# PSUM rings, emission order and first loads of an FFT filter with a mixture of experts behind it

## The chip, the cores and the metric

One core of one Trainium2 chip. The metric is the device time of one execution in microseconds (us); the time before is the median of three runs, 1523.91 us (1520.41 to 1524.9). The profile is of one more execution, of 1515.94 us.

## What is computed

The reference, cut to what matters:

```
x: (8, 2496, 256); filt_r, filt_i: (1249, 256); w_gate: (256, 8); w1: (8, 256, 1024); w2: (8, 1024, 256)
X = np.fft.rfft(x, axis=1)
Y = X * (filt_r + 1j * filt_i)
t = np.fft.irfft(Y, n=2496, axis=1).reshape(19968, 256)
logits = t @ w_gate
e = argmax(logits, axis=1); p = softmax(logits)[e]
out[row] = p * (relu(t[row] @ w1[e]) @ w2[e])       # for each row, its own expert
```

A filter by circular convolution along the sequence, then one expert of eight for each row of the result.

## The kernel before, in words

**The stages.** The sequence length is split as 2496 = 39 x 64, so a DFT is two small ones. The work of the first stage is cut into 16 units (u = 2 * batch + half of the 256 channels), and a unit into 5 steps, 80 steps t in all. `forward1(u, j)` (line 250; j = 0 to 5, six banks of columns) multiplies input columns by the 39-point table and leaves the result in T. A step is `spec1` (291, four transposes), `spec2` (305, the 64-point DFT), `filt_` (323, the product with the filter, on VectorE), `join` (336, real and imaginary parts, two instructions on GpSimd and two on VectorE) and `spec3` (348, the inverse 64-point DFT, copied to U by ScalarE).

When both units of a batch are through, the batch is **routed** (lines 481 to 614): `route1` and `route1b` take the gate's product twice (s = 0, 1), turn it round and copy it out on VectorE; `route2` to `route6` are a chain of small matmuls, exponentials, one-hot rows and prefix sums that ends in each row's place (`dest`) and its gate weight (`meta`). And it is **inverted**: for j = 0 to 10, `inv1` transposes (618) and ScalarE rounds the result (gh), `inv1b` takes the rest on VectorE (gq, 635), `inv2` multiplies three times into one PSUM bank and ScalarE copies it out (yt, 649 to 651), and `inv3` (654) adds the meta columns and scatters two groups of rows to the dispatch buffer xs with GpSimd.

Beside this, 16 chunks of **expert weights** are loaded, scaled and split in two f16 halves: `w_load`, `w_max` (VectorE), `w_turn` (a matmul), `w_top` (VectorE), `w_wide` (a matmul), `w_scale`, `w_hi` (ScalarE), `w_lo` (VectorE), `w_out` (to memory). The second stage (from line 912) runs the experts over blocks of 128 rows; `layer1` and `layer2` are its matmuls. It needs all the weights, and the rows dispatched so far.

**The order.** Nothing is scheduled by a tool: each call is entered with `at(key, f, ...)` (803), the list is sorted by key (1125), and the engines' queues are filled in that order. Each engine takes its own instructions strictly in that order. The unit of the keys is one step: `spec1(t)` has the key t, `spec2` t + 1.394, `spec3` t + 3.6. Line 821 has the distances, with `w` the key of the first weight chunk and `wp` the distance to the next. `RT` (822) has the ten links of the routing, counted from s0, the moment the batch is complete. The inverse begins `lead` after s0 and has a pair each 0.75 steps, with `inv1b` 0.4 and `inv2` 0.9 after `inv1`, and `inv3` 1.2 after it (times c, which is 0.6 in the last batch). The weights, the constants and x are loaded by SP's queue (`loadx` is 3 DMAs, `loadf` 8, or 12 for the first); lines 753 to 772 and then the list fill it.

**PSUM.** There are 8 banks. Pools turn round: an allocation waits until the tile that had the bank before has been read. Before, pF has 4 banks for forward1, spec1, spec2, spec3 and inv1; pY has 2 for inv2; pW has 1 for w_turn and w_wide; pD has 1 for the routing. In the last batch inv2 uses pF.

Of the kernel before, what the change touches and what calls it, by code (L numbers as in the profile page):

```python
# [9 lines left out]
F32 = mybir.dt.float32  # L10
# [7 lines left out]
PSUM = bass.MemoryType.PSUM  # L18
# [95 lines left out]
def tile_fft_moe(ctx, tc, x, filt_r, filt_i, w_gate, w1, w2, cst, out):  # L114
    nc = tc.nc
    B = x.shape[0]
# [7 lines left out]
    SEG = []  # L124
# [60 lines left out]
    with ExitStack() as fctx:  # L185
# [6 lines left out]
        wp = pool(name="wp", bufs=2)  # L192
        fp = pool(name="fp", bufs=1)
        rp = pool(name="rp", bufs=1)
        pF = pool(name="pF", bufs=4, space=PSUM)
# [2 lines left out]
        sctx = fctx.enter_context(ExitStack())  # L198
        early = lambda **k: sctx.enter_context(tc.tile_pool(reuse_waits="tile", **k))
        sp = early(name="sp", bufs=2)  # L200
        pY = early(name="pY", bufs=2, space=PSUM)
        pW = early(name="pW", bufs=1, space=PSUM)
        pA = pB = pC = pF

        cm = kp.tile([128, 20, 128], F32, name="cm")
        bm = kp.tile([128, 20, 128], F32, name="bm")
# [43 lines left out]
        def forward1(u, j):  # L250
            g0, g1 = BANKS[j]
            n = 0
            ps = pC.tile([128, 512], F32, name=f"f1_{u}_{j}", tag="pF")
            for g in range(g0, g1):
                m = GP if g < NG - 1 else N1
                nc.tensor.matmul(  # L256
                    ps[:, n : n + m],
                    lhsT=xt.pop((u, g))[:m],
                    rhs=a1[:m, :m],
                    start=True,  # L260
                    stop=True,
                )
                n += m
            (nc.scalar.copy if j in (0, 1, 2, 3, 5) else nc.vector.tensor_copy)(  # L264
                T[u % 2].rearrange("p r n -> p n r")[:, 3 * g0 : 3 * g0 + n // N1, :],
                ps[:, :n].rearrange("p (n r) -> p n r", r=N1),
            )
# [140 lines left out]
        def w_turn(e, i):  # L408

            wf, m = whs[e, i]  # L410
            ps = pW.tile([128, 512], F32, name=f"pw{e}_{i}", tag="pW")
            nc.tensor.matmul(ps[0:1, :128], lhsT=m[:, 2:3], rhs=ident, start=True, stop=True)
            whs[e, i] = (wf, m, ps)

# [3 lines left out]

        def w_wide(e, i):
            wf, m, ps = whs[e, i]  # L420
            ps = pW.tile([128, 512], F32, name=f"pv{e}_{i}", tag="pW")
            nc.tensor.matmul(ps[:, 0:1], lhsT=one, rhs=m[0:1, 0:1], start=True, stop=True)
            whs[e, i] = (wf, ps)

# [341 lines left out]
        ps = pD.tile([128, 512], F32, name="pwarm", tag="pD")  # L766
        for i in range(7):
            nc.tensor.matmul(ps, lhsT=warm[:, :128], rhs=warm, start=True, stop=True)
        for j in range(6):
            forward1(0, j)  # L770
            if j < 2:
                loadx(0, j + 4)
# [30 lines left out]
        def at(key, f, *a):  # L803
            work.append((key, f, a))
# [13 lines left out]
                    )  # L818


        K = {"s2": 1.394, "sr": 1.65, "si": 1.85, "s3": 3.6, "f": 0.063, "fd": 0.75, "w": 2.0, "wp": 4.3}
        RT = (0.0, 0.4, 0.45, 0.9, 1.3, 1.7, 2.2, 2.5, 2.9, 3.3)
        slow = lambda t: min(1.0, max(0.6, 1.0 - 0.06 * (t - 72)))
        for t in range(NT):
            u, it = divmod(t, 5)
            rho = slow(t)
            at(t, spec1, t)
            at(t + K["s2"] * rho, spec2, t)
            at(t + K["sr"] * rho, filt_, t)
            at(t + K["si"] * rho, join, t)  # L830
            at(t + K["s3"] * rho, spec3, t)
            if 0 < t < 5:
                at(max(t - 1.8, 0.05), loadf, t)
            if u + 1 < NU_ALL and it == 0:
                for j in range(6):
                    at(t + K["f"] + K["fd"] * j, forward1, u + 1, j)
            if u + 1 < NU_ALL and it == 0:
                for j in range(6):

                    n = 6 * (u + 1) + j - 4  # L840
                    v, i = divmod(n, 6)
                    at(5 * (v - 1) + K["f"] + K["fd"] * i + 0.02 if v else 0.01 + 0.02 * i, loadx, u + 1, j)
        for i in range(1, 5):
            if i > 1:
                at(0.1, loadk, bm, "bm", i, i + 1)
            at(0.1, loadk, cm, "cm", i, i + 1)

        PLACE = (80.0, 89.2, 109.2)
        done = []
        for b in range(B):  # L850
            rho = slow(10 * b + 9)
            s0 = 10 * b + 9 + K["s3"] * rho + 0.05
            c = 1.0 if b < B - 1 else 0.6
            for i, f in enumerate(
                (
                    (route1, 0),
                    (route1b, 0),
                    (route1, 1),
                    (route1b, 1),
                    (route2,),  # L860
                    (route3,),
                    (route4,),
                    (route4b,),
                    (route5,),
                    (route6,),
                )
            ):
                at(s0 + c * RT[i], f[0], b, *f[1:])
            lead = 2.0 if b < B - 1 else 1.3


            t = 10 * b + 20
            d = 0.35
            if b < B - 1:
                z = PLACE[0] - 2.85 if b == B - 2 else t + K["s3"] * slow(t) - 0.15
                d = min(0.75, (z - s0 - lead) / (NPAIR - 1))
            for j in range(NPAIR):
                z = s0 + lead + j * d
                at(z, inv1, b, j)
                at(z + 0.4 * c, inv1b, b, j)  # L880
                at(z + 0.9 * c, inv2, b, j)
                z = max(z + 1.2 * c, s0 + c * RT[9] + 0.1 + 0.9 * d * j)
                at(z, inv3, b, j)
            if b in [r for r, _, _ in SEG]:
                for s, v in enumerate(SEG):
                    if v[0] == b:
                        at(s0 + c * RT[9] + 0.2 + 0.1 * s, finish, s)
            done.append(z)
        for q in range(2 * E):
            e, i = divmod(q, 2)  # L890
            z = K["w"] + K["wp"] * q
            at(max(z - 3.2, 0.2 + 0.3 * q), w_load, e, i)
            for d, f, *a in (
                (0.0, w_max, 0),
                (0.12, w_max, 1),
                (0.9, w_turn),
                (1.0, w_top),
                (1.5, w_wide),
                (1.65, w_scale),
                (1.75, w_hi, 0),  # L900
                (1.85, w_hi, 1),
                (2.05, w_lo, 0),
                (2.2, w_lo, 1),
                (3.0, w_out),
            ):
                at(z + d, f, e, i, *a)
# [172 lines left out]
        for s, (r, m, n) in enumerate(SEG):  # L1079
            n *= m  # L1080
            a = PLACE[s]
            z = PLACE[s + 1] if s + 1 < len(SEG) else a + 0.5 * n
# [21 lines left out]
        for k in range(nu):  # L1104
            s, i, m, b0 = units[k]
            z, d, _ = tau[b0]
# [3 lines left out]
        for b in range(NB):  # L1110
            z, d, s = tau[b]
            y = max(opened(s) + 0.3, z - 1.1)
# [67 lines left out]
```

## Time and profile before

| | us |
|---|---|
| median of three runs | 1523.91 (1520.41 to 1524.9) |
| the profiled execution | 1515.94 |
| its span on the core | 1514.2 |
| what lies around the span | 1.74 |
| first step (spec1) at | 19.7 |
| sixth step (first of the second unit) at | 52.7 |
| last step (t = 79) at | 566.0 |
| mean granted TensorE clock | 0.959 |

The times of steps are the starts of their transposes (line 296) in the timeline. The profile names engines PE (TensorE matmuls), PEld (its weight loads), DVE (VectorE), ACT (ScalarE), POOL (GpSimd) and SPq (SP's DMA issues). A view of waits sums the idle time of one engine just before a group of its instructions and names what ended it; a windows view gives the busy time of each engine in a stretch.

### The profile page before, as it was taken

The numbers are of one execution on the slowest core, as the hardware profiler recorded it, in microseconds if no ns is written. First come the engines' busy times: TensorE is split into PE (matmuls) and PEld (weight loads), VectorE is DVE, ScalarE is ACT, GpSimd is POOL, SyncE is SP. The second block draws the span as 40 slices with busy tenths as digits, with TensorE's granted clock in tenths as the row PEclk, the third lists the DMA queues.
The fourth block names the chain that finished last, engine by engine and source line by source line (L and its number), as shares of the span: only waits on it lengthen the run. The fifth ranks groups of instructions, "written<-read, shape, count | busy, mean of one in ns | idle before, by whom it ended". The sixth has DMA issues, their size and how long they took to land.

```text
span 1514.2 us, 41597 instructions
## 1 busy us (share of the span) xinstructions
PE 1361.8 (90%) x15559; PEld 1212.1 (80%) x15559; DVE 879.1 (58%) x2550; ACT 850.0 (56%) x1440; POOL 480.7 (32%) x525
## 2 busy tenths in 40 slices
PE   6889888887888968679999998999999999999997
PEld 4767677676776747558999998899999899999997
DVE  0888777786768644535555554455555455555553
ACT  2457565655565544345656665566566566565664
POOL 1235565555554653442111111111111111111111
PEclk7899999999898998889999999999999999999999
DMA  6745444454443242227737339933733634534531
GB/s 182 217 143 164 149 149 130 150 164 140 129 151 120 60 163 65 83 69 191 197 79 181 81 76 306 264 77 75 184 76 100 155 80 123 136 77 96 164 77 44
DMA packets 200120, 199.19 MB, mean 132 GB/s; under 512 B 104707, under 2 KB 178100, under 8 KB 191724
## 3 DMA queue, kind: packets, MB, share of 16 engines
q1 hardware_dynamic: 180396, 153.80, 36.9%
q0 software_dynamic: 19520, 42.71, 10.1%
q8 instruction: 124, 2.03, 0.6%
q14 instruction: 80, 0.66, 0.1%
HBM read 347.54 MB, written 61.56 MB: 270 GB/s over the span
## 4 chain that ended last, share of the span: by engine, by line
PE 44%; DMA 4%; SPq 3%; issue 2%; DVE 1%; ACT 1%; POOL 0%; POOLq 0%; DVEq 0%
PE ph L1026 22%; PE po L1052 21%; DMA wb<-wscr 2%; DMA wa<-wscr 1%; SPq L935 1%; SPq L1013 1%; SPq L973 0%; DVE hl L1040 0%; POOL out_dram L158 0%; DMA xt<-xs 0%; SPq L943 0%; ACT hs L1032 0%; ACT hh L1034 0%; ACT xs L1005 0%; DVE xs L1006 0%
## 5 line engine op out<-in xcount | busy, mean ns | idle before, releaser
L1026 PE MATMUL ph<-xt,wa 128*128 128x128 f16 x7728 | 467.7, 220 | 22.2 <-issue 10.6
L1026 PEld LDWEIGHTS <-wa 128*128 128x128 f16 x7728 | 449.9, 99 | 34.3 <-issue 16.8
L1040 DVE TENSOR_TENSOR hl<-hs,hh 128x512 f16<-128x512 f32 x322 | 222.8, 692 | 370.7 <-ACT hh L1034 314.0
L1052 PE MATMUL po<-wb,hh 128*128 128x256 f16 x2576 | 431.7, 273 | 6.9 <-DMA wb<-wscr 3.7
L158 POOL DMA_INDIRECT out_dram<-ot,t x161 | 158.0, 982 | 693.7 <-DVE xs L1006 610.1
L1052 PE MATMUL po<-wb,hl 128*128 128x256 f16 x1288 | 351.1, 273 | 0.4 <-issue 0.4
L1052 PEld LDWEIGHTS <-hh 128*128 128x128 f16 x2576 | 244.8, 98 | 36.2 <-issue 5.8
L1032 ACT ACTIVATE hs<-ph 128x512 f32<-128x512 f32 x322 | 191.8, 596 | 107.8 <-PE ph L1026 93.1
L158 POOL DMA_INDIRECT xs<-yt,dest x176 | 185.1, 1052 | 109.9 <-issue 31.7
L1005 ACT ACTIVATE xs<-xb,s 128x256 f16<-128x256 f32 x161 | 81.8, 508 | 228.0 <-DVE s L995 223.2
L1034 ACT CAST hh<-hs 128x512 f16<-128x512 f32 x322 | 199.0, 618 | 10.2
L1052 PEld LDWEIGHTS <-hl 128*128 128x128 f16 x1288 | 126.0, 98 | 16.3 <-issue 1.3
L361 ACT COPY U<-pi 128x512 f32<-128x512 f32 (+1 forms) x80 | 87.6, 1095 | 91.5 <-PE pi L356 52.2
L256 PE MATMUL f<-a,x 117*128 117x117 f32 x704 | 109.1, 300 | 14.5 <-DMA x<-in_x_dram 12.7
L356 PE MATMUL pi<-cm,p 128*128 128x128 f32 (+1 forms) x640 | 98.6, 297 | 24.6 <-POOL p L345 13.4
L256 PEld LDWEIGHTS f<-a,x 117*128 117x128 f32 x704 | 99.9, 211 | 25.8 <-issue 12.7
L1006 DVE SCALAR_TENSOR_TENSOR xs<-xb,s,xs 128x256 f16<-128x256 f32 x161 | 78.5, 488 | 65.1 <-ACT xs L1005 55.2
L356 PEld LDWEIGHTS pi<-cm,p 128*128 128x128 f32 x640 | 85.2, 202 | 37.5 <-issue 18.5
L264 ACT COPY T<-f 128x468 f32<-128x468 f32 (+1 forms) x80 | 70.8, 885 | 58.7 <-PE f L256 56.7
L314 PE MATMUL px<-z,bm 128*64 128x128 f32 x1280 | 96.7, 298 | 3.0 <-ACT U L361 2.7
L345 POOL TENSOR_TENSOR p<-tr,ti 64x256 f32<-64x256 f32 x80 | 62.8, 785 | 107.3 <-DMA xs<-yt,dest 104.0
L344 POOL TENSOR_TENSOR p<-tr,ti 64x256 f32<-64x256 f32 x80 | 62.7, 784 | 104.8 <-DVE ti L331 95.0
(171 smaller groups left out, 1476.9 us busy)
## 6 DMA issues: line engine op xcount, KB each, us to landing
wb<-wscr SPq DMA_DIRECT2D x134, 1040.0 KB
wa<-wscr SPq DMA_DIRECT2D x134, 1024.0 KB
xb<-xs SPq DMA_DIRECT2D x161, 130.0 KB
x<-in_x_dram SPq DMA_DIRECT2D x240, 78.0 KB
wf<-in_moe_w_dram SPq DMA_DIRECT2D x32, 512.0 KB
wscr<-wh SPq DMA_DIRECT2D x8, 1040.0 KB
wscr<-wh SPq DMA_DIRECT2D x8, 1024.0 KB
xs<-yt,dest POOLq DMA_INDIRECT x176
```

Source lines behind the costliest of these rows:

```text
L158: nc.gpsimd.indirect_dma_start(out=dst, out_offset=bass.IndirectOffsetOnAxis(ap=idx, axis=0), in_=src, in_offset=None, bounds_check=bound, ...
L256: nc.tensor.matmul(ps[:, n : n + m], lhsT=xt.pop((u, g))[:m], rhs=a1[:m, :m], start=True, stop=True,)
L314: nc.tensor.matmul(ps[64 * a : 64 * a + 64, i, j], lhsT=bm[:, 4 * it + kk, 64 * i : 64 * i + 64], rhs=z[:, kk], start=True, stop=True,)
L356: nc.tensor.matmul(ps[:, o : o + n], lhsT=p[:, kk], rhs=cm[:, k, :n], start=True, stop=True)
L361: nc.scalar.copy(U[u % NU].rearrange("p n r -> p r n")[:, r0 : r0 + o // 64, :], ps[:, :o].rearrange("p (r n) -> p r n", n=N2),)
L1005: nc.scalar.activation(xs_[:, 0], xb[:, :D], AF.Copy, scale=sc)
L1006: nc.vector.scalar_tensor_tensor(xs_[:, 1], xb[:, :D], sc, xs_[:, 0], op0=ALU.mult, op1=ALU.subtract)
L1026: nc.tensor.matmul(ps[:, f], lhsT=w[:, p : p + 128], rhs=xt[:, r, c], start=(n == 0), stop=(n == 5))
L1032: nc.scalar.activation(s, ps, AF.Relu, scale=1.0 / B23)
L1034: nc.scalar.copy(hh, s)
L1040: nc.vector.tensor_tensor(hl, s, hh, op=ALU.subtract)
L1052: nc.tensor.matmul(ps, lhsT=h2[q][:, f % 4], rhs=wv[:, r, f], start=(f == 0 and n == 0), stop=(f == 7 and n == 2),)
```

## The change

Four things. PSUM: forward1, w_turn and w_wide move to pY, which has 3 banks, pW is gone, and pF's 4 banks serve spec1 to spec3 and inv1. Routing and inverse: for batches 0 to 5 the links of the routing are 1.5 times as far apart, the inverse starts 3.2 steps after s0 and not 2.0, and inv1b, inv2 and inv3 lie 0.5, 1.3 and 2.1 after inv1. Weights: the first chunk at step 6, the others 4.05 steps apart. The beginning: forward1 of the second unit is spread over steps 1.6 to 4.35, and tables, filter and x are issued in another order, with the first weight load at 2.8 (0.2 before).

```diff
--- before.py
+++ after.py
@@ -198,8 +198,7 @@
         sctx = fctx.enter_context(ExitStack())
         early = lambda **k: sctx.enter_context(tc.tile_pool(reuse_waits="tile", **k))
         sp = early(name="sp", bufs=2)
-        pY = early(name="pY", bufs=2, space=PSUM)
-        pW = early(name="pW", bufs=1, space=PSUM)
+        pY = early(name="pY", bufs=3, space=PSUM)
         pA = pB = pC = pF
 
         cm = kp.tile([128, 20, 128], F32, name="cm")
@@ -250,7 +249,7 @@
         def forward1(u, j):
             g0, g1 = BANKS[j]
             n = 0
-            ps = pC.tile([128, 512], F32, name=f"f1_{u}_{j}", tag="pF")
+            ps = pY.tile([128, 512], F32, name=f"f1_{u}_{j}", tag="pY")
             for g in range(g0, g1):
                 m = GP if g < NG - 1 else N1
                 nc.tensor.matmul(
@@ -408,7 +407,7 @@
         def w_turn(e, i):
 
             wf, m = whs[e, i]
-            ps = pW.tile([128, 512], F32, name=f"pw{e}_{i}", tag="pW")
+            ps = pY.tile([128, 512], F32, name=f"pw{e}_{i}", tag="pY")
             nc.tensor.matmul(ps[0:1, :128], lhsT=m[:, 2:3], rhs=ident, start=True, stop=True)
             whs[e, i] = (wf, m, ps)
 
@@ -418,7 +417,7 @@
 
         def w_wide(e, i):
             wf, m, ps = whs[e, i]
-            ps = pW.tile([128, 512], F32, name=f"pv{e}_{i}", tag="pW")
+            ps = pY.tile([128, 512], F32, name=f"pv{e}_{i}", tag="pY")
             nc.tensor.matmul(ps[:, 0:1], lhsT=one, rhs=m[0:1, 0:1], start=True, stop=True)
             whs[e, i] = (wf, ps)
 
@@ -818,7 +817,7 @@
                     )
 
 
-        K = {"s2": 1.394, "sr": 1.65, "si": 1.85, "s3": 3.6, "f": 0.063, "fd": 0.75, "w": 2.0, "wp": 4.3}
+        K = {"s2": 1.394, "sr": 1.65, "si": 1.85, "s3": 3.6, "f": 0.063, "fd": 0.75, "w": 6.0, "wp": 4.05}
         RT = (0.0, 0.4, 0.45, 0.9, 1.3, 1.7, 2.2, 2.5, 2.9, 3.3)
         slow = lambda t: min(1.0, max(0.6, 1.0 - 0.06 * (t - 72)))
         for t in range(NT):
@@ -833,17 +832,20 @@
                 at(max(t - 1.8, 0.05), loadf, t)
             if u + 1 < NU_ALL and it == 0:
                 for j in range(6):
-                    at(t + K["f"] + K["fd"] * j, forward1, u + 1, j)
+                    at(t + K["f"] + K["fd"] * j if u else 1.6 + 0.55 * j, forward1, u + 1, j)
             if u + 1 < NU_ALL and it == 0:
                 for j in range(6):
 
                     n = 6 * (u + 1) + j - 4
                     v, i = divmod(n, 6)
-                    at(5 * (v - 1) + K["f"] + K["fd"] * i + 0.02 if v else 0.01 + 0.02 * i, loadx, u + 1, j)
+                    z = 5 * (v - 1) + K["f"] + K["fd"] * i + 0.02
+                    if v < 2:
+                        z = 1.6 + 0.55 * i + 0.02 if v else 0.2 + 0.25 * j
+                    at(z, loadx, u + 1, j)
         for i in range(1, 5):
             if i > 1:
-                at(0.1, loadk, bm, "bm", i, i + 1)
-            at(0.1, loadk, cm, "cm", i, i + 1)
+                at(max(i - 1.9, 0.1), loadk, bm, "bm", i, i + 1)
+            at(max(i - 1.4, 0.15), loadk, cm, "cm", i, i + 1)
 
         PLACE = (80.0, 89.2, 109.2)
         done = []
@@ -851,6 +853,8 @@
             rho = slow(10 * b + 9)
             s0 = 10 * b + 9 + K["s3"] * rho + 0.05
             c = 1.0 if b < B - 1 else 0.6
+            v = 1.5 if b < B - 2 else c
+            y = (0.5, 1.3, 2.1) if b < B - 2 else (0.4 * c, 0.9 * c, 1.2 * c)
             for i, f in enumerate(
                 (
                     (route1, 0),
@@ -865,8 +869,8 @@
                     (route6,),
                 )
             ):
-                at(s0 + c * RT[i], f[0], b, *f[1:])
-            lead = 2.0 if b < B - 1 else 1.3
+                at(s0 + v * RT[i], f[0], b, *f[1:])
+            lead = 3.2 if b < B - 2 else 2.0 if b < B - 1 else 1.3
 
 
             t = 10 * b + 20
@@ -877,14 +881,14 @@
             for j in range(NPAIR):
                 z = s0 + lead + j * d
                 at(z, inv1, b, j)
-                at(z + 0.4 * c, inv1b, b, j)
-                at(z + 0.9 * c, inv2, b, j)
-                z = max(z + 1.2 * c, s0 + c * RT[9] + 0.1 + 0.9 * d * j)
+                at(z + y[0], inv1b, b, j)
+                at(z + y[1], inv2, b, j)
+                z = max(z + y[2], s0 + v * RT[9] + 0.1 + 0.9 * d * j)
                 at(z, inv3, b, j)
             if b in [r for r, _, _ in SEG]:
-                for s, v in enumerate(SEG):
-                    if v[0] == b:
-                        at(s0 + c * RT[9] + 0.2 + 0.1 * s, finish, s)
+                for s, part in enumerate(SEG):
+                    if part[0] == b:
+                        at(s0 + v * RT[9] + 0.2 + 0.1 * s, finish, s)
             done.append(z)
         for q in range(2 * E):
             e, i = divmod(q, 2)
```

## Rows read from the trace of the kernel before

**Rows 1.** The page: the span, and its part 1, busy us by engine.

```profile
span 1514.2 us, 41597 instructions
...
PE 1361.8 (90%) x15559; PEld 1212.1 (80%) x15559; DVE 879.1 (58%) x2550; ACT 850.0 (56%) x1440; POOL 480.7 (32%) x525
```

**Rows 2.** Windows, stretches of 50 us: length, then busy us, clock, DMA share, GB/s.

```profile
0.00:50.00 50.00, 31.26 (x171) 25.49 (x171) 11.86 (x22) 11.71 (x15) 6.55 (x17) 0.69 0.65 182
...
550.00:600.00 50.00, 35.33 (x356) 29.51 (x357) 21.91 (x68) 22.48 (x37) 20.45 (x25) 0.83 0.44 140
600.00:650.00 50.00, 34.79 (x345) 29.05 (x342) 26.35 (x115) 19.33 (x37) 19.94 (x21) 0.81 0.28 79
```

**Rows 3.** Windows by tens of steps (PE, PEld, DVE, ACT, POOL), two of seven, and the sum.

```profile
138.80:206.10 67.30, 58.67 (x499) 47.90 (x500) 50.93 (x113) 40.41 (x60) 37.61 (x43) 0.97 0.47 146
...
418.20:492.40 74.20, 63.02 (x497) 50.66 (x495) 56.53 (x137) 42.63 (x62) 38.01 (x41) 0.91 0.41 129
...
sum 507.40, PE 430.74 PEld 349.48 DVE 378.60 ACT 292.36 POOL 271.17; mean PE 61.53 PEld 49.93 DVE 54.09 ACT 41.77 POOL 38.74
```

**Rows 4.** Waits of PE from 50 to 560 us: us in total, times, longest.

```profile
PE py L649 <- DVE gq L635: 13.4, 9, 3.2
PE pi L356 <- POOL p L345: 9.8, 7, 2.7
PE pt L296 <- ACT U L361: 7.5, 9, 2.2
PE pw L412 <- DVE wm L400: 5.5, 3, 2.3
PE py L649 <- ACT yt L651: 5.1, 3, 2.1
PE pl L528 <- DVE gl L517: 4.1, 3, 1.7
...
PE px L314 <- ACT U L361: 2.7, 3, 1.1
PE pp L564 <- DVE oh L555: 2.5, 2, 1.4
PE pt L296 <- ACT T L264: 2.4, 2, 1.7
...
PE plw L487 <- DVE gl L517: 0.9, 1, 0.9
```

**Rows 5.** Waits of DVE from 50 to 560 us.

```profile
DVE tr L331 <- POOL p L345: 20.8, 9, 4.2
DVE gl L510 <- PE f L256: 16.4, 4, 4.6
```

**Rows 6.** Timeline of the beginning: start, us, engine, what, count, idle before.

```profile
17.32 0.38 SPq L281 DMA_DIRECT2D ff<-in_filt_r_dram  x1
...
20.55 0.42 SPq L287 DMA_DIRECT2D ff<-in_filt_i_dram  x1
...
35.59 2.03 PE L256 MATMUL f<-a,x 117*128 117x117 f32 x8 [4.38 <-DMA x<-in_x_dram]
...
37.59 1.17 SPq L241 DMA_DIRECT2D x<-in_x_dram  x3
...
40.58 1.22 DVE L389 TENSOR_REDUCE wm<-wf 128x1 f32<-128x1024 f32 x1 [8.76 <-DMA wf<-in_moe_w_dram]
...
43.77 0.59 PE L412 MATMUL pw<-ident,wm 128*1 128x128 f32 x2 [4.25 <-DVE wm L400]
```

**Rows 7.** Groups of instructions from 52 to 650 us: busy us, mean ns, idle before.

```profile
L460 DVE SCALAR_TENSOR_TENSOR wh<-wf,ws,wh 128x1024 f16<-128x1024 f32 x32 | 41.9, 1325 | 11.6 <-ACT wh L455 9.8 <-ACT U L361 1.2 <-issue 0.3
```

## The prediction, made before the changed kernel was run

> **What bounds the kernel now.** I read the page first, then windows, then the waits of PE and VectorE in the first stage, last the timeline of the first 50 us. PE is busy 1361.8 of 1514.2 us [rows 1], so what can be won is PE's idle time, 152 us. It lies at the beginning and in the first stage: the windows show 18.7 us of idle PE in the first 50 us and 14.7 and 15.2 us in the two stretches of the hand-over to the experts [rows 2], and 76.7 us between 52.6 and 560 us [rows 3]. The change touches nothing after step 80, so the expert stage is taken as it is, only earlier.
>
> In the first stage no engine is full. Over 507.4 us PE is busy 430.7, its weight loads 349.5 (69%), VectorE 378.6 (75%), ScalarE 292.4, GpSimd 271.2 [rows 3]. Ten steps take 67.3 us where the inverse begins and 74.2 us later, with nearly the same count of matmuls (499 and 497) [rows 3]: one step is some 7 us, of which about 6 are PE's. It is a pipeline of five queues, each in strict order, that loses time because one queue reaches an instruction before another has delivered. So the list of PE's waits is what to read, and of each wait whether the change puts distance, or a bank, in front of it [rows 4].
>
> **The change, part by part.** All sums are against the profiled execution, span 1514.2 us [rows 1] and 1.74 us around it, 1515.94 us. The median is 1523.9, 8 us more; I carry the difference over to the median.
>
> **The beginning.** SP issues the eight pieces of one filter block from 17.32 to 20.97 us [rows 6], 0.46 us each, and it is issuing nearly all the time: the beginning is paced by how many issues stand ahead of what is needed. Before, PE waits 4.38 us for x of the second unit at 35.6 us, and then 4.25 us at 43.8 us for the maximum of the first weight chunk, whose load ended VectorE's wait at 40.6 us [rows 6]. The second wait goes: the first weight load moves behind the tables, and w_turn to step 6.9. The first becomes another one: counted from the list, 75 issues come up to the last x of the second unit before, the last at 38.8 us [rows 6], and 91 after, because three filter blocks and the constants now stand ahead of it. Sixteen more at 0.46 us give 46 us for the last x issue, 7 us later. But after it little is left to do: one forward1, a spec2, a spec3 and the sixth spec1, some 5 us. Before, between the wait that ends at 43.8 us and the sixth spec1 at 52.7 us, PE worked 9 us. So the sixth step starts between 47 (the constants' small issues cost less than 0.46) and 54 us; I take 49, that is **-4 us** (ends -6 and +2).
>
> **One weight chunk more in the full stage.** Before, chunk 0 was worked off in the beginning, under DMA waits. Now all 16 lie between steps 6 and 70. On VectorE one chunk is two maxima at 1.22 us [rows 6] and two w_lo at 1.325 us [rows 7], with small ones 6 us. VectorE has a quarter of its time free, so I take **+2 us** (0 to +6).
>
> **Inverse, more distance.** inv1b to inv2 goes from 0.5 to 0.8 steps: about 2 us more for ScalarE's rounding and VectorE's subtraction to arrive before PE needs gq. PE waited 13.4 us for gq, 9 times, at most 3.2 us [rows 4]. Most are within reach of 2 us: **-10 us** (0 to -13.4). The cover is other PE work that stands between, spec2 and spec3 of two more half steps.
>
> **PSUM.** Per ten steps pF gave out 30 tiles to spec1 to spec3, 12 to forward1, 11 to inv1: 53 over 4 banks, a bank comes round after 0.75 steps. After, 41: 0.98 steps, so 1.6 us more. PE's waits for ScalarE to empty such banks are 7.5, 2.7 and 2.4 us [rows 4], 12.6 in all: **-9 us** (0 to -12.6). In return pY has 12 forward1, 11 inverse and 5 weight tiles on 3 banks, round after 1.07 steps, where inv2 alone had 1.8. PE's wait for ScalarE's copy of yt is 5.1 us already [rows 4]; it is the nearest row, and I take **+2 us** (0 to +5 for the same wait doubled).
> The Trainium skill (Perfetto Trace Analysis, Optimization Strategy) says that the same gap coming back on the engine that should be saturated can mean too few PSUM buffers. By that reading all four bank waits, 17.7 us, would go and pY would cost nothing, 8 to 10 us better than my two terms; the rows agree only for a quarter of PE's idle time, since most of its gaps end on VectorE or GpSimd data.
>
> **Routing.** The links come 1.5 times as far apart. PE waited 4.1 us for gl ahead of route2, 2.5 us for the one-hot rows ahead of route4, 0.9 us at the second route1 [rows 4], 7.5 us over seven batches, of which six get the new distance: **-6 us** (0 to -7.5). VectorE's own wait at gl, 16.4 us in four visits [rows 5], does not shrink by this: the transposes and the copy are emitted in one call, so distance between them stays nil. The last two batches keep their old distances, and so the hand-over keeps its idle PE [rows 2].
>
> **The tail of batch 5.** Its inverse now ends at step 75.45, not 73.35, across the routing of batch 6 (from 72.65) and its pairs, packed 0.25 steps apart. Stretches near there are already the emptiest [rows 2]: **+2 us** (0 to +5).
>
> **The sum.** The three groups of PE waits give -25 us. Not all is kept: untouched are PE's wait for GpSimd's part of join, 9.8 us, and for the weights' maximum, 5.5 us [rows 4], and VectorE's wait for GpSimd's read of tr, 20.8 us [rows 5]. GpSimd in order is what comes late next. I keep four fifths, -20, since VectorE at 75% and PE's loads at 69% leave room. With -4 and +6: **-18 us**; I add 2 us for VectorE's waits on the same copies, which PE's rows don't count, and say -20: 1524 - 20 = **1504 us**.
>
> **Rivals.**
> (a) *The waits move.* VectorE and GpSimd are the true pace, PE's gaps only show it. For it: VectorE's share is the highest of the elementwise engines [rows 3], its 20.8 us for GpSimd stay [rows 5], and no instruction is removed. Against it: VectorE is idle 129 us in the stage. Then only the beginning counts, less the extra chunk: -4 + 2 = -2, 1522 us.
> The Trainium skill (Perfetto Trace Analysis, Identifying the Most-Contended Engine) would have the most occupied engine relieved first, with PE judged by its weight loads; by its measure that is VectorE here, which gets no less work, and the result would be this rival's.
> (b) *pY is the new stall, and it is slower.* w_turn's and w_wide's tiles are now in the ring of forward1 and inv2, and both are freed by VectorE, behind its queue. Three allocations can fall into some 0.6 steps, 4 us; VectorE already lags PE by that much, with gl waits up to 4.6 us [rows 5]. It decides where VectorE's lag is over those 4 us in most chunks: then each of 32 weight tiles costs PE about what an average wait for a py bank costs now, 5.1 / 3 = 1.7 us [rows 4], 54 us at worst; at half of them 27 us, against -20 gained: 1531 us.
> (c) *More than the waits.* PE's rows hide lost time within "busy" (430.7 busy, 349.5 of loads [rows 3]); with looser links ten steps could all take the 67.3 us of the early stretch [rows 3], not up to 74.2: some 30 us over the stage, 45 with the rest: 1478 us.
>
> **Chances.** Forecast 0.50, (c) 0.20, (a) 0.14, (b) 0.16. About 0.3%, 4.6 us, is what a measurement of this kernel can tell from no change. The forecast and (c) are nearly all faster: 0.70; (a) and the weak edge of the forecast are within 0.3%: 0.14; (b) is slower: 0.16. The range reaches to (c)'s end and into (b): 1472 to 1532. Its lower end is all of the gains at their bounds (-6 - 13.4 - 12.6 - 7.5 = -39.5) and a third more by (c); its upper end is (b) with its 27 us.
>
> **What would show it.** Right: the sixth spec1 near 49 us with no PE wait for wm in the first 50 us; in PE's waits gq and ScalarE's U under 5 us each, gl under 2; ten steps in 66 to 70 us; the last spec1 20 us earlier. Wrong: pw, pv or f waiting on VectorE or ScalarE in PE's list (b); the same length of ten steps with the idle time put down to POOL p and VectorE (a); a first x wait of over 8 us at the beginning; or a hand-over after step 80 that gives the gain back.

## The result, and the profile after

The changed kernel takes 1507.77 us (median of 6 runs, 1503.16 to 1515.08) where the kernel before took 1523.28 us in the same set (6 runs): ratio 0.9914, 95% interval 0.9885 to 0.9943 (the two medians alone give 0.9898, inside that interval). The forecast was 1504 us. A second measurement, told below in the third set of experiments, gave 0.9900 (0.9859 to 0.9940). The three sets of experiments ran on three chips. The kernel before took 1520 us in the first and 1491 to 1492 us in the two others; so ratios are compared, and times only within one set.

The profiled execution has a span of 1501.4 us, 12.8 us less than before [rows 1]. A profile is of one execution, here 4.6 us under the median of its kernel, and the profile before is 8 us under its own; so a few us between two profiles can be chance. The starts of the transposes in the timeline tell where the 12.8 us were won:

| start of | before | after | difference |
|---|---|---|---|
| step 5 | 52.7 | 49.9 | -2.8 |
| step 10 | 76.0 | 70.3 | -5.7 |
| step 20 | 138.8 | 131.3 | -7.5 |
| step 40 | 274.2 | 265.9 | -8.3 |
| step 50 | 343.8 | 333.9 | -9.9 |
| step 60 | 418.2 | 399.5 | -18.7 |
| step 79 | 566.0 | 553.2 | -12.8 |
| first expert block | 577.8 | 564.0 | -13.8 |

More than half is there by step 20, and little is added up to step 50. The ten steps from 50 win another 8.8 us, and the nineteen from step 60 give 5.9 us back. The hand-over and the experts give back 1 us.

PE's waits from 50 to 560 us in the changed kernel (us in total, times, longest). Line numbers are one less than before, so L344 is what was L345:

```profile
PE pi L355 <- POOL p L344: 29.4, 29, 3.7
PE pi L355 <- POOL p L343: 8.2, 6, 4.8
PE pt L295 <- ACT U L360: 6.2, 7, 1.9
PE py L648 <- DVE gq L634: 6.1, 3, 3.7
PE plw L486 <- DVE gl L516: 5.9, 4, 2.1
PE pw L411 <- DVE wm L399: 4.7, 4, 3.2
...
PE pp L563 <- DVE oh L554: 1.1, 1, 1.1
PE py L648 <- ACT yt L650: 1.0, 1, 1.0
```

Against [rows 4], most of the waits that the change aimed at are shorter: gq 13.4 to 6.1, yt 5.1 to 1.0, the bank waits of pt and px 12.6 to 6.2, gl ahead of route2 from 4.1 to nothing. One is longer: the second route1 (plw) waits for gl 5.9 us and not 0.9. But the first two rows are new in size: spec3 waits for GpSimd's part of join 37.6 us in 35 visits, where it was 9.8 us in 7. These two rows grew by 27.8 us; the rows that shrank gave up some 22.

The beginning, first the waits of PE in the first 52 us, then SP's last issues for x of the second unit and PE's fifth step and the sixth:

```profile
PE f L255 <- DMA x<-in_x_dram: 13.2, 6, 4.0
PE f L255 <- DMA ff<-in_filt_r_dram: 2.5, 1, 2.5
```

```profile
40.80 1.17 SPq L240 DMA_DIRECT2D x<-in_x_dram  x3
...
43.42 2.02 PE L255 MATMUL f<-a,x 117*128 117x117 f32 x8 [3.97 <-DMA x<-in_x_dram]
45.24 1.06 PE L295 MATMUL pt<-ident,T 128*128 128x128 f32 x4
...
49.88 0.60 PE L295 MATMUL pt<-ident,T 128*128 128x128 f32 x4
```

The wait for the weights' maximum [rows 6] is gone from the beginning; x is still waited for. The last three x issues of the second unit go out from 40.80 to 41.97 us, and the sixth step begins at 49.88 us.

The windows of tens of steps, the ten from step 50 before, and then three of six after (length, then busy PE, PEld, DVE, ACT, POOL):

```profile
343.80:418.20 74.40, 61.30 (x500) 50.03 (x501) 52.43 (x117) 39.96 (x60) 41.26 (x46) 0.93 0.44 140
```

```profile
131.30:199.80 68.50, 60.67 (x495) 50.16 (x496) 52.63 (x115) 41.91 (x61) 38.38 (x43) 0.93 0.48 154
...
333.90:399.50 65.60, 56.92 (x497) 46.39 (x498) 52.30 (x113) 39.26 (x59) 38.87 (x44) 1.00 0.52 158
399.50:475.30 75.80, 60.86 (x499) 49.34 (x497) 58.35 (x145) 42.83 (x63) 40.55 (x44) 0.93 0.41 128
```

Up to step 60 ten steps take 66 to 69 us, where they took 67 to 74; the ten from step 60 take 75.8 us, where they took 74.2 [rows 3].

### The profile page after: what moved, and what is told of

Read it like the earlier page. It is cut to its first block, busy times and chain, and to the rows that moved or that the text cites. A ratio compares the mean times of both kernels' runs of the same rounds, so it can differ in the third digit from the quotient of the medians.

```text
span 1501.4 us, 41577 instructions
## 1 busy us (share of the span) xinstructions
PE 1352.8 (90%) x15559; PEld 1207.7 (80%) x15559; DVE 875.9 (58%) x2550; ACT 848.4 (57%) x1440; POOL 479.5 (32%) x525
## 4 chain that ended last, share of the span: by engine, by line
PE 44%; DMA 5%; issue 2%; SPq 2%; DVE 1%; ACT 1%; POOL 0%; POOLq 0%; ACTq 0%; DVEq 0%
PE ph L1030 23%; PE po L1056 22%; DMA wb<-wscr 2%; DMA wa<-wscr 2%; DMA xt<-xs 1%; SPq L939 1%; DVE hl L1044 1%; SPq L1017 0%; POOL out_dram L158 0%; ACT hh L1038 0%; ACT hs L1036 0%; SPq L977 0%; ACT xs L1009 0%; DVE xs L1010 0%; DVE m L995 0%
## 5 line engine op out<-in xcount | busy, mean ns | idle before, releaser
L255 PE MATMUL f<-a,x 117*128 117x117 f32 x704 | 106.7, 295 | 16.4 <-DMA x<-in_x_dram 13.9
L255 PEld LDWEIGHTS f<-a,x 117*128 117x128 f32 x704 | 96.4, 207 | 25.7 <-issue 14.9
L313 PE MATMUL px<-z,bm 128*64 128x128 f32 x1280 | 93.3, 291 | 1.9 <-ACT z L301 1.5
L344 POOL TENSOR_TENSOR p<-tr,ti 64x256 f32<-64x256 f32 x80 | 61.9, 774 | 101.1 <-DMA xs<-yt,dest 97.8
```

Source lines behind the costliest of these rows:

```text
L255: nc.tensor.matmul(ps[:, n : n + m], lhsT=xt.pop((u, g))[:m], rhs=a1[:m, :m], start=True, stop=True,)
L313: nc.tensor.matmul(ps[64 * a : 64 * a + 64, i, j], lhsT=bm[:, 4 * it + kk, 64 * i : 64 * i + 64], rhs=z[:, kk], start=True, stop=True,)
```

## The experiments

Twelve runs in three sets of four. My theory after the result: each part of the change does what it says, but the steps from 20 on are paced by GpSimd's queue, so that a wait removed elsewhere comes back ahead of spec3. The rival was (a): only the beginning counts. A third reading was that VectorE or PE is the pace, and GpSimd only the last name on the list. The lists of waits below are of the time from 50 to 545 us.

What made GpSimd suspect is its own timeline (changed kernel, 276 to 300 us):

```profile
279.09 1.10 POOL L158 DMA_INDIRECT xs<-yt,dest  x1 [0.30 <-issue]
280.26 0.72 POOL L343 TENSOR_TENSOR p<-tr,ti 64x256 f32<-64x256 f32 x1
282.33 0.73 POOL L344 TENSOR_TENSOR p<-tr,ti 64x256 f32<-64x256 f32 x1 [1.35 <-DMA xs<-yt,dest]
...
292.57 0.99 POOL L158 DMA_INDIRECT xs<-yt,dest  x1 [0.30 <-issue]
293.62 0.72 POOL L343 TENSOR_TENSOR p<-tr,ti 64x256 f32<-64x256 f32 x1
295.86 0.73 POOL L344 TENSOR_TENSOR p<-tr,ti 64x256 f32<-64x256 f32 x1 [1.52 <-DMA xs<-yt,dest]
```

Between join's two halves GpSimd stands still, 1.35 us from 280.98 to 282.33 and 1.52 us from 294.34 to 295.86, and what ends it is a scatter's DMA: the scatters issued just before must land first. In steps 14 to 69 of the timeline, 13 joins with no scatter before them have 0.07 us between the halves; 27 with two scatters have 1.66 us on average, 16 with four 2.46 us (before: 0.08 in 11, 2.04 in 28, 1.99 in 17). GpSimd's waits of this kind were there before the change too (first line, from 0 to 560 us), and in the changed kernel they add up to the second line (50 to 545 us):

```profile
POOL p L345 <- DMA xs<-yt,dest: 96.9, 49, 4.6
```

```profile
POOL p L344 <- DMA xs<-yt,dest: 92.5, 49, 4.6
```

From the end of the last scatter's issue, 280.19 us, to the second half are 2.14 us, and they stand inside GpSimd's queue. The Trainium skill (DMA: Bandwidth & Descriptors, Anatomy of one DMA — SWDGE (gpsimd) path) puts some 2 us of fixed cost on such a DMA, most of it the receipt of the write. The trace agrees with the size if it is counted from the end of the issue (3.24 us from its start); what the time goes into no run here shows.

The list of instructions with their waits shows what holds GpSimd (changed kernel, step 74; DMASW are the scatters' eight semaphores, the counters on which a landing is told):

```
L158 DMA xs<-yt_10,dest [waits DVE,Activation,Pool]
L158 DMA xs<-yt_10,dest
L343 TENSOR_TENSOR p<-tr,ti 64x256 [waits DVE,PE]
L344 TENSOR_TENSOR p<-tr,ti 64x256 [waits DMASW6,DMASW5]
L158 DMA xs<-yt_0,dest [waits DVE,Activation,Pool]
```

The wait hangs on GpSimd's instruction that reads tr and ti in the upper 64 partitions: in listings with the halves exchanged it moves with it, and if GpSimd reads the lower partitions only it is not there. The scatters read yt and dest, not tr or ti, so no data asks for it; why the framework puts it there stays open. Without it each scatter waits instead for the one eight before it, four pairs of the inverse back.

**The parts alone, and the changed kernel without that wait** (first set; kernel before 1520.45 us).

```diff
 only_psum:  only pY = 3 banks, pW gone, forward1, w_turn, w_wide in pY
 only_order: only v, y and lead (routing x 1.5, inverse 0.5 / 1.3 / 2.1, lead 3.2) for b < B - 2
 only_begin: only "w": 6.0, "wp": 4.05, forward1 at 1.6 + 0.55 * j, loadx and loadk keys
 join_low_after: the changed kernel and
-                e[1 - a].tensor_tensor(p[hi, k], tr[q, 1], ti[q, 0], op=ALU.add)
+                e[a].tensor_tensor(p[hi, k], tr[q, 1], ti[q, 0], op=ALU.add)
```

> The kernel before with the PSUM rings of the change alone. If bank waits cost what PE's rows said: PE's waits for ScalarE's copies ahead of pt and px (12.6 us before) fall under 7 us, and the time falls by 3 to 7 us (ratio 0.995 to 0.998). If GpSimd's part of join sets the pace of steps 20 to 60, the waits move to pi <- POOL p, and the time stays within 3 us. If the common ring of forward1, inv2 and the weights' tiles is a stall (rival b), PE waits on pw, pv or f appear and the time rises by 5 us or more.

Measured: 1513.55 us, ratio 0.9961 (0.9936 to 0.9987). As expected, pt's wait for U fell to 3.5 us and rival (b) did not show: w_turn, w_wide and forward1 wait for no bank there. The wait for join grew by 3 us, from 9.8 to 12.8. gq stayed at 14.5 us, as it should without the new distances:

```profile
PE py L648 <- DVE gq L634: 14.5, 8, 3.2
PE pi L355 <- POOL p L344: 12.8, 10, 3.1
PE pg L622 <- ACT U L360: 6.7, 5, 2.9
```

> The kernel before with the larger distances in routing and inverse alone (batches 0 to 5). By the forecast's terms: gq and gl waits of PE fall from 17.5 us to under 8 us and the time by 5 to 12 us (ratio 0.992 to 0.997). If GpSimd's queue sets the pace: the step length from 20 to 60 stays 6.9 to 7.0 us, pi <- POOL p takes the place of gq, and the time stays within 3 us. If the later end of batch 5's inverse costs, the hand-over is 2 to 5 us later against step 70.

Measured: 1507.06 us, ratio 0.9908 (0.9878 to 0.9937): as good alone as the whole change was in its own set. gq's wait left the list and the second route1's wait for gl took its place, 9.3 us:

```profile
PE plw L487 <- DVE gl L517: 9.3, 6, 2.8
PE pt L296 <- ACT U L361: 8.0, 9, 1.7
PE pi L356 <- POOL p L345: 7.1, 8, 1.6
```

Steps 20 to 59 went from 7.00 to 6.70 us each, against GpSimd as a hard limit. But see the second measurement below.

> The kernel before with the new order of loads, the spread forward1 of the second unit, and the later weights alone. If the beginning is what counts (rival a): step 5 near 50 us, step 20 some 7 us earlier than before (131.5), and the whole time 6 to 9 us less (ratio 0.994 to 0.996). If the extra weight chunk eats it, step 20 is early but step 60 is not, and the time is within 3 us.

Measured: 1511.78 us, ratio 0.9948 (0.9926 to 0.9970), 8.7 us less and more than the -2 us that I had given the beginning with the weights. Where the 8.7 us come from is not clear. The sixth step starts at 49.7 us, as expected, but step 20 at 136.0 us and not at 131.5: only 2.8 of the 7.5 us that the whole change has won by step 20 are the beginning's alone.

The three alone sum to 6.9 + 13.4 + 8.7 = 29.0 us; together they gave 15.5 in the set of the result. So they overlap, and in this set rival (a) falls: the two other parts alone are faster as well.

> The changed kernel, with join's two GpSimd instructions both reading the lower 64 partitions and VectorE's two the upper: same work, but the second GpSimd half no longer waits for the scatters just issued to land. If GpSimd's queue is what took the rest of the gain: the idle time between the two halves (1.7 to 2.5 us after scatters) falls to 0.1 us, pi <- POOL p from 37.6 us to under 10, steps 20 to 60 from 6.76 us each to 6.2 or less, and the time falls by 15 to 30 us against the changed kernel. If VectorE or PE is the pace, the waits only change names: steps 20 to 60 stay over 6.6 us and the time stays within 5 us.

Measured: 1475.94 us, ratio 0.9696 (0.9668 to 0.9724), 32 us less than the changed kernel's 1507.8 us in its own set and just over what I had expected. Between the halves are now 0.06 us in all 56 joins of steps 14 to 69, GpSimd's part of join ends 4.4 us after its inputs and not 9.4 (means over steps 20 to 59), and a step takes 6.45 us and not 6.76. The waits of PE:

```profile
PE py L648 <- DVE gq L634: 10.3, 6, 2.6
PE pw L411 <- DVE wm L399: 7.6, 6, 2.8
...
PE pi L355 <- POOL p L344: 7.1, 2, 5.7
```

The 37.6 us for join are 7.1 us in two visits. No work was taken away or added: VectorE's two instructions of join stayed at 0.42 us, and GpSimd's two took 0.74 and 0.81 us (medians) after 0.72. So the landing waits were a pace of this stage, and VectorE was not. The step length that I had named, 6.2 us, was too hopeful: gq and the weights' maximum come next.

**Without one part, and the kernel before without the wait** (second set, another chip; kernel before 1490.63 us). The three are the changed kernel less one part; the fourth is the kernel before with the one line of join above.

> The kernel before with join's GpSimd halves both from the lower partitions, and nothing else. If GpSimd's waits for landings hid the change's gain, the kernel before gains less from them than the changed one did (32 us): it had 2.7 us of slack between join and spec3 in steps 20 to 60, so 10 to 22 us, to 1498 to 1511; the change is then worth 22 us or more on top (1476 measured). If the two gains merely add, it falls by 31 to 33 us to about 1489, and the change is worth its 13 to 15 us there too.

Measured: 1450.97 us, ratio 0.9722 (0.9688 to 0.9756), 39.7 us less. The expectation was wrong: the kernel before gains from it at least as much as the changed one, although PE's list had only 9.8 us for join [rows 4]. The wait hurt in other places: GpSimd's late read of tr held VectorE 20.8 us [rows 5], and that row is down to 1.0 us here. What else GpSimd's lateness put off is not measured.

> The changed kernel with routing and inverse at their old distances (PSUM and beginning kept). Alone, PSUM gave 0.39% and the beginning 0.52%. If they add: 0.991, about 1507, as good as the whole change. If they share the same slack before GpSimd: 0.994 to 0.996, 1511 to 1514.

Measured: 1489.56 us, ratio 0.9981 (0.9957 to 1.0005).

> The changed kernel with the old PSUM rings (order and beginning kept). If PSUM's 0.39% is its own: 1512 to 1515. If it is spent behind GpSimd's queue when the other two parts are there: within 2 us of the whole change, 1506 to 1510.

Measured: 1484.60 us, ratio 0.9952 (0.9925 to 0.9979).

> The changed kernel with the old beginning and the old weight keys (PSUM and order kept). If the early gain (5.7 us at step 10 in the profile) is kept to the end, 1512 to 1516. If it is taken back by GpSimd later, within 3 us of the whole change: 1506 to 1511.

Measured: 1491.60 us, ratio 1.0004 (0.9980 to 1.0027), though PSUM and order alone had given 0.39 and 0.92% in the first set. Its list of waits has the same name on top as the whole change:

```profile
PE pi L355 <- POOL p L344: 22.6, 15, 3.4
PE pt L295 <- ACT U L360: 9.2, 11, 1.7
PE pw L411 <- DVE wm L399: 7.5, 4, 3.0
```

None of the three pairs reached what I expected of it. Against the whole change in the next set, 0.9900, they are 0.81, 0.52 and 1.04% slower, some 12, 8 and 16 us; the 0.52%, without PSUM, is not clear of the two intervals. So here the order and the beginning are each missed, where in the first set the parts overlapped. That left open whether the whole holds on another chip.

**The whole again, beside the order alone and both kernels without the wait** (third set, a third chip; kernel before 1491.98 us).

> The changed kernel once more, beside the three below on one chip. Two of its parts together gave 0.995 to 1.000 on a chip where the kernel before takes 1491 us, the whole 0.991 on one where it takes 1523. If the parts all run into GpSimd's queue, the whole gives 0.990 to 0.996 here, whichever chip it is. If the first measurement was a chip's matter, 0.998 to 1.002.

Measured: 1477.16 us, ratio 0.9900 (0.9859 to 0.9940). The change is worth 14.8 us here too.

> Routing and inverse distances alone once more. If the order is what carries the change and the rest is lost behind GpSimd: within 0.3% of the whole change in the same call. If the parts add: 0.4 to 0.9% slower than the whole change.

Measured: 1491.72 us, ratio 0.9997 (0.9969 to 1.0024). The same kernel that gave 0.9908 gives nothing here. Its profile has 7.10 us a step from 20 to 59, where the first set's had 6.70, and between join's halves stand 2.14 and 2.39 us after two and four scatters, where there were 1.80 and 2.05. The profiled execution is the slowest of the twelve, 7.5 us above their median, so part of this is that one execution. PE waits for join again:

```profile
PE pi L356 <- POOL p L345: 24.5, 16, 4.2
PE pw L412 <- DVE wm L400: 7.6, 5, 2.6
PE pt L296 <- ACT U L361: 7.4, 9, 2.2
```

What one part is worth did not carry over. Longer landings are a part of it at most: from step 20 to 59 GpSimd's waits between the halves sum to 72.6 us here and to 63.8 in the first set, 8.8 us apart, while the stretch is 15 us longer. And the kernel before has 65.0 us of them in its profile, nearly as much as the order alone in the first set, at 0.3 us a step more. The whole held in both sets.

> The kernel before without GpSimd's waits for landings in join, beside the next on one chip: 0.970 to 0.975 of the kernel before.

Measured: 1451.32 us (1449.05 to 1457.71), ratio 0.9722 (0.9683 to 0.9760), as in the set before.

> The changed kernel without those waits. If they hid the change's gain, it is now 1.2 to 2% faster than the run before it (0.953 to 0.960 of the kernel before). If both remove the same lost time, it is within 0.4% of the run before it (0.967 to 0.975).

Measured: 1444.36 us (1443.77 to 1447.66), ratio 0.9675 (0.9640 to 0.9711). It is nearest to the second expected case: without the landing waits the change is worth 1451.3 - 1444.4 = 7.0 us, 0.5% where I had said at most 0.4%, with runs that do not overlap; with them it is worth 14.8. About half of the change's gain and the removal of the wait are thus the same lost time, and half is its own. The windows of this kernel, two of five:

```profile
195.30:257.50 62.20, 57.11 (x501) 47.73 (x500) 54.80 (x115) 40.31 (x60) 41.31 (x44) 0.97 0.51 163
...
383.30:452.00 68.70, 60.56 (x499) 49.99 (x497) 59.90 (x146) 42.63 (x63) 41.91 (x46) 0.93 0.47 151
```

Ten steps take 61.5 to 64.3 us up to step 60 and VectorE is busy 88% (54.80 of 62.20). With the change and the one line in join it is the fastest version of the study, 3.3% under the kernel before.

## Why the prediction was right, point by point

**The number and its side** held: -20 us forecast, -15.5 and -14.8 measured, against a range from -52 to +8. That the sum came out is in part luck: several terms were off, some too high and some too low.

**The beginning** (-4, and +2 for the chunk). The sixth step is at 49.88 us, as forecast at 49, but by two errors that cancel. The last x issue ends at 41.97 us, not at 46: 87 issues stand up to it and not 91, and SP had not been issuing all the time before (the eight pieces of a filter block took 5.6 us from 30.8 us on, 3.7 us in the changed kernel). And from that issue to the sixth step it takes 7.9 us, not 5. The moved weight chunk cost nothing that can be seen: in only_begin, steps 5 to 79 take 509.8 us, before 513.2. In the first set the part gave 8.7 us alone, not 2; in the second, with PSUM, the two gave 0.2%, which is not clear of nothing.

**Inverse** (-10): gq's wait fell by 7.3 us, from 13.4 to 6.1. **PSUM** (-9 + 2): the bank waits of pt and px fell by 6.4 us, and pY, which I had charged with 2 us, gave 4.1 us: yt's wait went from 5.1 to 1.0 us. All of that wait stood from 544 to 555 us, in the packed pairs of batch 6, where forward1 and the weights no longer ask for banks; so three banks served one user there better than two. The same wait is 1.0 us with the rings alone (only_psum) and 4.8 without them (no_psum). So of the four bank waits, 17.7 us, 10.5 went, and pY cost nothing that the list shows. The other reading in the prediction, by which all four waits go, lies 10.7 us from my two terms, not 8 to 10, and was the nearer one for pY.

**Routing** (-6) failed as a term. The wait for gl ahead of route2 went, 4.1 us, but the wait of the second route1 for gl grew from 0.9 to 5.9 us: in RT that call still stands 0.05 x 1.5 steps behind route1b, and the distance was put elsewhere. VectorE's own wait at gl, which I had said would not shrink, did: the 16.4 us behind PE's f [rows 5] are gone from its list, and 4.8 us for pgl and pt are left.

**"I keep four fifths"** is the step that was wrong in kind. By the terms the stage from step 5 to 79 was to be 14 to 16 us shorter; it is 10 us shorter in the profiles (513.2 to 503.3), while join's wait took 27.8 us more and the waits that fell gave some 22. Steps 20 to 59 went from 7.00 to 6.76 us each. I named the right successor, "GpSimd in order is what comes late next", and gave it a fifth. The 96.9 us that GpSimd itself waited for landings I had not read as a wait of the program; shown is now that this wait, and not GpSimd's work, was a limit, since the same work without it is 2.3 to 2.8% faster (0.9675 against 0.9900, and 0.9722 against 1).

**The tail of batch 5** (+2). From step 60 to 79 the changed kernel needs 153.7 us and the kernel before 147.8, 5.9 us more. The six profiles with the new distances (and the landing waits) have 146.7 to 154.3 us there, the four with the old ones 144.5 to 147.8; so a cost there is likely, and nearer to 4 us than to 2. Where the new distances pay is the ten steps from 50: 63.6 to 66.2 us in five of those six profiles and 70.5 in the last (only_order_again), against 71.0 to 74.4 in the four.

**Signs.** The sixth step and the missing wait for wm came as I had said. gq (6.1) and U (6.2) stayed just over the 5 us that I had named, gl (5.9) over 2, and the last spec1 came 12.8 us earlier, not 20. The sign of (a) showed in part: the idle time is put down to POOL p.

**Rivals.** (a), *the waits move*, is right for GpSimd and wrong for VectorE: the reading that VectorE is the pace fell with join_low. That only the beginning counts fell in the first set, where the other parts alone were faster. In the later sets it is not settled: the order alone (0.9997) and the order with PSUM (1.0004) gave nothing, as (a) would have it, but the beginning with one of them (0.9981 and 0.9952) did not give the whole 0.9900. Its time, 1522 us, was 14 us off. (b) was not seen: of w_turn, w_wide and forward1 the longest wait for a bank of pY is forward1's in no_begin, 1.0 us in two visits. The row that I gave for VectorE lagging behind PE (gl, 4.6 us [rows 5]) is VectorE waiting for PE, so it did not speak for (b). (c) came close in size only for the kernel without the wait, by another mechanism.

Not settled: why pairs of parts give 0 to 0.5% in the second set, and the order alone nothing in the third, where single parts gave 0.4 to 0.9% in the first.

## What to carry to other kernels

In strictly ordered queues the wait that is longest on the busiest engine's list need not be the one that sets the pace: look at who is next in line, and at what its own idle time ends on. An idle gap that ends on the landing of a DMA that the next instruction doesn't read is worth a look at the list of waits before any distance is tuned; here one exchanged operand was worth nearly three times the whole change (40.7 us against 14.8 in the third set). And the parts of this schedule change, which run into one common queue, neither added up nor carried over to another chip, so measure parts together and on more than one.

## What was not expected of the hardware

The kernel before takes 1520 us on one chip and 1491 on the two others. Most of the difference lies in the hand-over: from the eighth to the eleventh expert block the changed kernel needs 665.6 - 619.2 = 46 us in the profile of the result and 631.5 - 608.7 = 23 us in that of the third set. It goes with the set and not with the kernel: the six profiles of the result and the first set have 45 to 47 us there, the eight of the two later sets 22.8 us each. In the first six, ScalarE's copy of yt stands still for 15 to 16 us in one piece, in the others there is no such row. The row names a matmul (ph) here and nothing that the profile knows in the other five, so what it waited for stays open.

```profile
ACT yt L650 <- PE ph L1030: 15.8, 1, 15.8
```
